# Early operands, value order, later value loads and wide weight decoding in an attention and FFN kernel

## The chip, the cores and the metric

The kernel runs on one core of one Trainium2 chip. The metric is the device time of one execution in microseconds. The engines have short names in the profile: PE is TensorE's matmul, PEld its weight load, DVE VectorE, ACT ScalarE, POOL GpSimd, SP the engine that issues DMAs.

## The reference: what is computed

Eight batches of eight heads, 576 tokens of 64 dimensions each, causal attention with a bias from a running sum; then a feed-forward network (FFN) with an ELU over all 4608 tokens (q comes scaled by 6.41 and k by 6.42):

```
scores = q @ k.T / sqrt(64)
cum    = cumsum(max(s, 0))                   # per batch and head
bias   = -(cum[:, None] - cum[None, :])
scores = where(causal, -1e9, scores + min(bias, 0))
p      = exp(scores - max(scores));  attn = p / (sum(p) + 1e-9)
x      = concat_heads(attn @ v)              # 4608 x 512
h      = x @ w_in                            # 512 x 2048
g      = where(h > 0, h, exp(min(h, 0)) - 1)
out    = g @ w_out                           # 2048 x 512
```

Two weight matrices reach the device as 64-bit numbers, and the kernel itself makes 32-bit numbers of them.

## The kernel before: how the work is tiled and ordered

**The plan.** All work is first recorded as operations (class Plan, L87). An operation has one or more ways (an engine and a cost in ns), what it reads and writes, and a priority. Plan.issue then puts them in order: the operation that can start first by the plan's costs, and among equals the one of lower priority number. It so fixes the order of every engine's instructions before the run, and each engine keeps it. Buffers of one tag are handed out in turn (N_ST = 2 buffers of tag st for keys of the early pairs, N_QS = 2 of tag qs for their queries); a load into a buffer waits until the work that used it before is done. In the first 60 us of the plan's time (FILL_T) transposes of the identity into a tile named scratch fill PE's gaps (L1569 to L1575): such a filler goes in when the next operation would start 350 ns later or more. They calculate nothing.

**The stages.** First decay_sums (L466) makes the running sums, in the tile aux, which is also written to aux_dram in DRAM. Then the early pairs (class Low): the first 320 tokens of batches 0 to 2, each batch as four pairs of heads, in native fp32. prepare_low (L824) loads keys (kl), queries (ql), and one row of decay into the keys' tile; scoring_low (L856) makes the scores (sc, L1101), masks them and takes the row's maximum on DVE (L1104), the exponential on ACT (L1109), the reciprocal of the sums (L1115) and the scaling by it (L1119 to L1124); weighing_low (L895) transposes the probabilities (trl, L904 and L925), copies them (tl) and multiplies by the values vs (avl). The result x_first is, for the first 256 tokens and a second chunk of 256, the operand of a native fp32 FFN (h at L1398, o at L1428).

After that come units: a pair of heads of a later batch with all 576 tokens, or the last 256 tokens of batches 0 to 2 (cut units); there are 20 full ones and 12 cut ones. Scores are again L1101. weighing (L1212) multiplies by the values, which are split in high and low 16-bit parts: heads (L1259) writes the products av (L1265), the two heads of the pair on the two 64-column halves of the array, three terms for each block of 128 keys, two for the last. In a full unit a block of keys meets 512, 448, 320, 192 and 64 columns of queries, in a cut one 256, 256, 256, 192 and 64. Meanwhile the FFN of the finished tokens runs in 16-bit parts (h at L1457, o at L1517), between the products of the units.

**Values.** group_values (L961) loads the values va of a full batch's pairs, four loads, each followed by its largest absolute value (peak, L595: DVE at L598, or ACT at L601 where a spare tile is at hand). Their priority is the unit's, less V_AHEAD.

**Weights.** Sixteen blocks of w_in and of w_out, 512 columns each. load_unit (L666) loads one (512 KB) into the ring w_raw of N_RAW = 4 places, ACT alters the high words (L684), DVE the low words (L687), DVE joins both to fp32 in wv (L690), and peak finds the largest; ACT's way uses the raw tile as its output. weight_scales makes a scale from four blocks' peaks, and split_unit (L699) splits wv in a scaled 16-bit high part (L414, L415) and a rest (DVE, L707).

The lines of load_unit that the change widens:

```
op(prio, [("ACT", act_s(512), lambda: act.activation(
    raw(1).bitcast(F32), raw(1).bitcast(F32), ...
op(prio, [("DVE-SB", 430.0, lambda: dve.tensor_scalar(
    raw(0), raw(0), 2.0**-29, 7.0, ALU.mult, ALU.min))],
```

Of the kernel before, what the change touches and what calls it, by code (L numbers as in the profile page):

```python
# [17 lines left out]
P = 128  # L18
# [17 lines left out]
V_AHEAD = 60  # L36
# [11 lines left out]
N_QS = 2  # L48
N_CUT, CUT = 3, 2
# [3 lines left out]
N_FREE = 0  # L53

# [288 lines left out]
def kernel(  # L343
# [114 lines left out]
    def low_keys(tag):  # L458

        k = plan.buf(sb, [P, 2, LOW], F32, f"kl_{tag}", tag="st", bufs=N_ST)  # L460
        return k, [("Pool-M", pool_1(2 * LOW), lambda: pool.memset(k.v[HB:], 0.0))]


    k_first, cleared = low_keys("first")

    def decay_sums():  # L466
# [25 lines left out]
        op(-10, [("DVE-SB", 2700.0, first)], [], [(aux, "row"), (k_first, "sums")])  # L492
# [70 lines left out]
    w_raw = plan.buf(sb, [P, N_RAW, 512, 2], U32, "w_raw", tag=f"wp_{NG - 1}")  # L563
# [11 lines left out]
    groups = [(b, False) for b in range(N_CUT, B)] + [(b, True) for b in range(N_CUT)]  # L575
    A_LOW, A_W = 0, N_CUT * (NP + 1)
# [3 lines left out]
    S_GROUP = S_LOW + 2 * N_CUT  # L580
# [85 lines left out]
    def load_unit(f, kind, src):  # L666

        prio = W_PRIO[f // W_GROUP] + f % W_GROUP
        a, n = src.shape[1], f"{'io'[kind]}{f}"
        place, value = weight(f, kind)  # L670
        at = A_W + f // W_GROUP * 2 * (W_GROUP + 1) + kind * (W_GROUP + 1) + f % W_GROUP
        r = (2 * f + kind) % N_RAW

        def raw(m):
            return w_raw.v[:, r, :, m]

        if wide:
            load(prio, lambda: w_raw.v[:, r].rearrange("p (a n) t -> p a (n t)", a=a),
                 lambda: src.bitcast(U32), [], [(w_raw, (r, 0)), (w_raw, (r, 1))], P * 4096,
                 urgent if f >= N_FREE else ())  # L680
# [3 lines left out]
            op(prio, [("ACT", act_s(512), lambda: act.activation(  # L684
                raw(1).bitcast(F32), raw(1).bitcast(F32),
                AF.Prelu, scale=2.0**-112, alpha=2.0**32))], [], [(w_raw, (r, 1))])
            op(prio, [("DVE-SB", 430.0, lambda: dve.tensor_scalar(  # L687
                raw(0), raw(0), 2.0**-29, 7.0, ALU.mult, ALU.min))],
               [], [(w_raw, (r, 0))])
# [966 lines left out]
```

## Time and profile before

| | us |
|---|---|
| runs | 1048.58, 1047.91, 1046.78 |
| median | 1047.91 |
| the profiled execution | 1049.47 |
| its span in the profile | 1047.7 |
| TensorE busy in the span | 1029.5 |
| VectorE busy in the span | 843.2 |

The granted clock of TensorE is 1.00 throughout. The span is the time from the first to the last instruction on the core; 1.77 us of the profiled execution lie around it. A row of the timeline gives the start, the length, engine, line, output and inputs, the count, and in brackets the wait before it; matmuls follow each other at less than the length shown, since they are pipelined and their ends are modelled. A row of groups gives the count, then busy time and mean length of one in ns, then idle time before them.

### The profile page before, as it was taken

Reading aid. Unit: us, or ns where it says so; the run is one execution under the profiler, and the core shown is the slowest. Engines: PE = TensorE matmul, PEld = TensorE weight load, DVE = VectorE, ACT = ScalarE, POOL = GpSimd, SP = SyncE. Lnnn points to the kernel's source line nnn. Section 1 sums busy time; section 2 is a strip of 40 time slices with the busy share of each in tenths; the row PEclk is TensorE's granted clock in tenths of the full one; section 3 lists DMA queues with packets and bytes.
Section 4 is the critical chain, followed back from the end, with each engine's and each line's share of the span. In section 5 each row is a group of like instructions: output and inputs, shape, how many; then the busy total and the mean of one; then the engine's idle time right before and its main releaser. Section 6 shows DMA issues by size and latency. Waiting matters only on the chain.

```text
span 1047.7 us, 21529 instructions
## 1 busy us (share of the span) xinstructions
PE 1029.5 (98%) x7161; PEld 710.2 (68%) x7161; DVE 843.2 (80%) x2142; ACT 619.8 (59%) x1475; POOL 428.7 (41%) x707
## 2 busy tenths in 40 slices
PE   9899999999999999999999999999999999999998
PEld 7556566667667676666676766666666676767665
DVE  7899958978898888789878998888888888885333
ACT  4788555655666666556676656656655566654232
POOL 4322415424545465446534555643433444441000
PEclk9999999999999999999999999999999999999999
DMA  7778025655666756658655855674666655663000
GB/s 235 247 227 240 26 74 142 131 148 115 139 129 147 171 122 129 134 122 174 128 132 119 186 129 124 137 175 94 147 131 155 131 130 123 142 108 73 1 21 21
DMA packets 277823, 137.76 MB, mean 131 GB/s; under 512 B 211768, under 2 KB 255056, under 8 KB 277712
## 3 DMA queue, kind: packets, MB, share of 16 engines
q1 hardware_dynamic: 277712, 136.39, 56.2%
q8 instruction: 57, 0.93, 0.4%
q14 instruction: 54, 0.44, 0.2%
HBM read 70.22 MB, written 9.88 MB: 76 GB/s over the span
## 4 chain that ended last, share of the span: by engine, by line
PE 83%; DVE 10%; DMA 3%; issue 2%; POOL 1%; ACT 1%; SPq 1%; POOLq 0%; DVEq 0%
PE h L1457 29%; PE o L1517 28%; PE sc L1101 9%; PE av L1265 5%; PE o L1428 4%; PE h L1398 4%; PE trl L925 1%; DVE p L1160 1%; PE scratch L1574 1%; PE avl L941 1%; DVE p L1104 1%; DMA vs<-in_vb_dram 1%; DVE peaks L598 1%; DVE wv L690 1%; DVE v L988 1%
## 5 line engine op out<-in xcount | busy, mean ns | idle before, releaser
L1457 PE MATMUL h<-x,wp 128*128 128x256 f16 x3072 | 380.6, 273 | 0.2 <-DVE x L1362 0.2
L1517 PE MATMUL o<-wp,gg 128*128 128x512 f16 x1536 | 362.1, 379 | 0.2 <-DVE gg L1496 0.2
L1457 PEld LDWEIGHTS <-wp 128*128 128x128 f16 x3072 | 286.6, 98 | 61.9 <-issue 7.5
L1517 PEld LDWEIGHTS <-gg 128*128 128x128 f16 x1536 | 144.9, 98 | 147.5 <-issue 2.8
L1109 ACT ACTIVATE p<-p,mn 128x192 f32<-128x192 f32 (+1 forms) x232 | 144.1, 621 | 73.0 <-DVE mn L1104 69.8
L1160 DVE SCALAR_TENSOR_TENSOR p<-p,sm,p 128x512 f16<-128x512 f32 (+3 forms) x221 | 159.8, 748 | 3.2 <-POOL p L1152 1.9
L1474 ACT ACTIVATE g<-h,cs 128x512 f32<-128x512 f32 x128 | 87.7, 685 | 109.1 <-PE h L1457 108.1
L1152 POOL TENSOR_SCALAR p<-p,sm 128x64 f16<-128x64 f32 (+3 forms) x125 | 81.1, 656 | 106.9 <-DVE sm L1115 70.0
L1104 DVE CUSTOM_DVE_ANT_0 p<-sc,maskw 128x192 f32<-128x192 f32 (+1 forms) x232 | 109.4, 481 | 18.2 <-PE sc L1101 15.9
L1491 ACT ACTIVATE gg<-h,wc 128x512 f16<-128x512 f32 x117 | 80.0, 684 | 68.0 <-DVE h L1487 67.2
L1101 PE MATMUL sc<-kh,qs 128*128 128x192 f32 (+2 forms) x272 | 112.3, 416 | 3.0 <-DVE mn L1104 3.0
L1496 DVE SCALAR_TENSOR_TENSOR gg<-h,wc,gg 128x512 f16<-128x512 f32 x128 | 95.5, 746 | 17.9 <-ACT gg L1491 17.4
L1487 DVE SCALAR_TENSOR_TENSOR h<-g,cs,h 128x512 f32<-128x512 f32 x128 | 96.2, 752 | 12.0 <-ACT g L1479 8.2
L1483 DVE TENSOR_SCALAR g<-g 128x512 f32<-128x512 f32 x77 | 36.2, 470 | 62.7 <-ACT g L1474 62.5
L1101 PE MATMUL sc<-k,q 128*128 128x192 f32 (+2 forms) x272 | 83.6, 310 | 0.6 <-DMA q<-qs 0.5
L1156 ACT ACTIVATE p<-p,sm 128x512 f16<-128x512 f32 (+3 forms) x104 | 59.0, 586 | 15.8 <-DVE sm L1115 14.9
L402 POOL TENSOR_SCALAR qs<-stq 128x512 fp32r<-128x512 f32 (+1 forms) x44 | 24.5, 558 | 100.9 <-PE sc L1101 66.2
L1101 PEld LDWEIGHTS sc<-kh,qs 128*128 128x128 f32 x272 | 51.6, 190 | 19.1 <-DVE mn L1104 4.7
L1398 PE MATMUL h<-x_first,wv 128*128 128x256 f32 x256 | 62.5, 382 | 0.6 <-ACT x_first L429 0.6
L1428 PE MATMUL o<-wv,gg 128*128 128x512 f32 x128 | 62.4, 595 | 0.0
L1265 PE MATMUL av<-T,v 128*64 128x256 f16 (+5 forms) x896 | 60.6, 286 | 0.2 <-DMA k<-aux_dram 0.2
L1265 PEld LDWEIGHTS <-v 128*64 128x64 f16 x896 | 44.9, 110 | 23.5 <-issue 8.6
(182 smaller groups left out, 1458.7 us busy)
## 6 DMA issues: line engine op xcount, KB each, us to landing
stk<-in_kT_dram SPq DMA_DIRECT2D x64, 288.0 KB
va<-in_vb_dram SPq DMA_DIRECT2D x32, 320.0 KB
stq<-in_qT_dram SPq DMA_DIRECT2D x40, 256.0 KB
w_raw<-in_w_in_dram SPq DMA_DIRECT2D x16, 512.0 KB
w_raw<-in_w_out_dram SPq DMA_DIRECT2D x16, 512.0 KB
out_dram<-ost SPq DMA_DIRECT2D x32, 256.0 KB
q<-qs SPq DMA_DIRECT2D x40, 128.0 KB
T<-p SPq DMA_TRANSPOSE x208
```

The source lines that it names most:

```text
L1101: pe_.matmul(view(sc.v[:, :cw]), l, r, start=n == 0, stop=n == len(pairs) - 1)
L1104: op(prio, [("DVE", 84 + dve_p(cw), lambda i=i, sc=sc: dve.tensor_tensor_reduce(pt.v[:, i * cw : (i + 1) * cw], sc.v[:, :cw], mv(i * cw, c ...
L1109: op(prio, [("ACT", 480 + w / 1.2, lambda: act.activation(pt.v[:, :w], pt.v[:, :w], AF.Exp, bias=mn.v[:, n - 1 : n], scale=-1.0, accum_out ...
L1160: ("DVE-SB", dve_2(n), lambda part=part: dve.scalar_tensor_tensor(part(t16, 1), own(part), sm.v[:, r], part(t16, 0), ALU.mult, ALU.subtract)),
L1265: pe_.matmul(av.v[w.h * HB : (w.h + 1) * HB, dst], w.values.v[:, w.h, kb, v], part(w, kb, m), start=kb == 0 and m == 0 and v == 0, stop=kb ...
L1398: op(main(ch), [("PE", pe4(TC), lambda m=m, c=c: pe_.matmul(hp.v[:, m], weight(2 * fp + m, 0)[1]()[:, c * P : (c + 1) * P], x_first.v[:, c ...
L1428: op(main(ch), [("PE", pe4(DM), lambda i=i, m=m: pe_.matmul(acc[i].v, gg.v[:, m, i * P : (i + 1) * P], weight(2 * fp + m, 1)[1](), start=f ...
L1457: pe_.matmul(hp.v[:, m], weight_part(f, 0, part)[1]()[:, c * P : (c + 1) * P], x.v[:, xx, c, o : o + TC], start=(c == 0 and i == 0), stop= ...
L1474: op(side, [("ACT", act_c(2 * TC) + 90, lambda: act.activation(gt.v, flat(hp.v), AF.Exp, scale=by(BACK)))], [hp, (cs[ch], g)], [gt])
L1487: op(side, [("DVE", dve_b(2 * TC), lambda: dve.scalar_tensor_tensor(flat(hp.v), gt.v, by(MINUS if sign[0] else FIRST), flat(hp.v), ALU.mul ...
L1496: op(side, [("DVE", dve_b(2 * TC), lambda: dve.scalar_tensor_tensor(flat(gg.v[:, 1]), flat(hp.v), down(), flat(gg.v[:, 0]), ALU.mult, ALU. ...
L1517: pe_.matmul(acc[i].v, gg.v[:, a, m, i * P : (i + 1) * P], weight_part(2 * fp + m, 1, part)[1](), start=(first and m == 0 and k == 0), sto ...
```

## The change

Six things are altered:

- Pairs 2 and 3 of batch 0 have their keys, queries and decay row in one tile of their own, early (of tag va), so that they are loaded at the start and wait for no buffer. Pairs 1 to 3 take the decay row from aux in SBUF; before, 2 and 3 took it from aux_dram.
- V_AHEAD is 30 in place of 60.
- A block of w_in and its block of w_out are decoded together, 1024 columns to an instruction, in a ring of two such blocks. The largest values come from one DVE reduction of both, or from two ACT instructions whose output goes to a tile w_abs, no longer to the raw tile.
- Blocks f and f + 1 of a kind are split together, 1024 columns to an instruction.
- The terms of av are written in alternating lengths, short then long, a long one last.
- N_WHOLE = N_CUT and N_URGENT = 1 name numbers that stood there already.

```diff
-V_AHEAD = 60
+V_AHEAD = 30
...
+N_EARLY, N_AUX, N_URGENT = 2, 4, 1
...
+    early = plan.buf(sb, [P, 2 * N_EARLY, 2 * LOW], F32, "early", tag="va", bufs=2)
+
+    def low_operands(n, tag, q_tag=True):
+        if 2 <= n < 2 + N_EARLY:
+            at = 2 * (n - 2)
+            return ((lambda part: (early, (n, part))), (lambda: early.v[:, at].rearrange("p (h t) -> p h t", h=2)),
+                    (lambda: early.v[:, at + 1]))
         k = plan.buf(sb, [P, 2, LOW], F32, f"kl_{tag}", tag="st", bufs=N_ST)
+        q = plan.buf(sb, [P, 2 * LOW], F32, f"ql_{tag}", tag="qs", bufs=N_QS)
...
-    w_raw = plan.buf(sb, [P, N_RAW, 512, 2], U32, "w_raw", tag=f"wp_{NG - 1}")
+    w_raw = plan.buf(sb, [P, N_RAW // 2, 2, 512, 2], U32, "w_raw", tag=f"wp_{NG - 1}")
+    w_abs = plan.buf(sb, [P, 512], F32, "w_abs")
...
+    def load_block(f, srcs):
...
-            op(prio, [("ACT", act_s(512), lambda: act.activation(
+            op(prio, [("ACT", act_s(1024), lambda: act.activation(
                 raw(1).bitcast(F32), raw(1).bitcast(F32),
-                AF.Prelu, scale=2.0**-112, alpha=2.0**32))], [], [(w_raw, (r, 1))])
-            op(prio, [("DVE-SB", 430.0, lambda: dve.tensor_scalar(
-                raw(0), raw(0), 2.0**-29, 7.0, ALU.mult, ALU.min))],
-               [], [(w_raw, (r, 0))])
-            op(prio, [("DVE-SB", 700.0, lambda: dve.scalar_tensor_tensor(
+                AF.Prelu, scale=2.0**-112, alpha=2.0**32))], [], highs)
+            op(prio, [("DVE-SB", 700.0, lambda: dve.tensor_scalar(
+                raw(0), raw(0), 2.0**-29, 7.0, ALU.mult, ALU.min))], [], lows)
+            op(prio, [("DVE-SB", 1240.0, lambda: dve.scalar_tensor_tensor(
                 value().bitcast(U32), raw(1), 3, raw(0),
...
+        ways = [("DVE", 140 + 1.04 * 1024, lambda: dve.tensor_reduce(
+            peaks.v[:, cols[0] : cols[1] + 1 : W_GROUP + 1], value(), mybir.AxisListType.X, ALU.max,
+            apply_absolute_value=True))]
+        def both():
+            for kind, col in enumerate(cols):
+                act.activation(w_abs.v, value()[:, kind], AF.Abs, accum_out=peaks.v[:, col : col + 1])
...
+    def split_units(f, kind):
...
+        scaled(prio, 1024, lambda: part(0), value, lambda: scales.v[:, col], [*places, (scales, at)], highs)
+        op(prio, [("DVE-SB", dve_2(1024), lambda: dve.scalar_tensor_tensor(
+            part(1), value(), scales.v[:, col], part(0), ALU.mult, ALU.subtract))],
+           [*places, (scales, at), *highs], lows)
...
-            src = aux if (b, j) == (0, 1) else aux_dram
+            src = aux if n < N_AUX else aux_dram
...
         def heads():
+            terms = [(kb, m, v) for kb in range(last + 1)
+                     for m, v in (((0, 0), (1, 0), (0, 1)) if kb < last else ((0, 0), (0, 1)))]
+            order, rest = terms[:1], sorted(terms[1:], key=lambda t: -columns(t[0]))
+            final = rest.pop(0)
+            while rest:
+                order.append(rest.pop())
+                if rest:
+                    order.append(rest.pop(0))
+            order.append(final)
...
-                for kb in range(last + 1):
+                for n, (kb, m, v) in enumerate(order):
                     dst = slice(wq - columns(kb), wq)
-                    for m, v in ((0, 0), (1, 0), (0, 1)) if kb < last else ((0, 0), (0, 1)):
-                        for w in pair:
```

The order of the engines' instructions changes with it. In a full unit the columns of the terms now run 512, 64, 512, 64, 448, 192, 448, 192, 448, 192, 320, 320, 320, 512. Fillers are 120 in number, 142 before. Three places, before and after.

SP, the loads behind the first pair's; va are full units' values, w_raw the weights, early the operands of pairs 2 and 3. Before:

```order
L390 DMA kl_1_131<-in_kT_dram 64x2x320
L390 DMA ql_1_139<-in_qT_dram 64x640
L390 DMA vs<-in_vb_dram 128x448
L390 DMA va_156<-in_vb_dram 128x640 x4
L390 DMA kl_1_131<-aux 1x2x320
L390 DMA aux_dram<-aux 64x576 x2
L390 DMA kl_2_232<-in_kT_dram 64x2x320
L390 DMA ql_2_239<-in_qT_dram 64x640
L390 DMA aux_dram<-aux 64x576
L390 DMA w_raw<-in_w_in_dram 128x4x256
```

The four va loads stand ahead of pair 2's operands (kl_2, ql_2). After, from the same place on SP:

```order
L391 DMA kl_1_131<-in_kT_dram 64x2x320
L391 DMA ql_1_139<-in_qT_dram 64x640
L391 DMA early<-in_kT_dram 64x2x320
L391 DMA early<-in_qT_dram 64x640
L391 DMA early<-in_kT_dram 64x2x320
L391 DMA early<-in_qT_dram 64x640
L391 DMA vs<-in_vb_dram 128x448
L391 DMA kl_1_131<-aux 1x2x320
L391 DMA aux_dram<-aux 64x576
L391 DMA early<-aux 1x2x320
```

The four operand loads of pairs 2 and 3 took the place of the four va loads, and the weights' loads moved down behind the rows of decay.

PE, from the last scores of pair 1 (sc_1_4) to the transposes of its probabilities (trl_1). Before:

```order
L1101 MATMUL sc_1_4_0_363<-kl_1_131,ql_1_139 128x320
L941 MATMUL avl_0_313<-tl_0_301,vs 64x64 x2
L1574 MATMUL scratch<-ident 128x128 x6
L1398 MATMUL h_0_391<-x_first,wv_366 128x256
L1574 MATMUL scratch<-ident 128x128 x21
L1101 MATMUL sc_2_0_0_431<-kl_2_232,ql_2_239 128x128
L904 MATMUL trl_1_434<-ident,pl_1_303 128x128
```

Pair 2's first scores stand behind 27 fillers and a product of the FFN. After, between the same two places on PE:

```order
L1141 MATMUL sc_1_4_0_345<-kl_1_131,ql_1_139 128x320
L981 MATMUL avl_0_298<-tl_0_288,vs 64x64 x2
L1141 MATMUL sc_2_0_0_355<-early 128x128
L1623 MATMUL scratch<-ident 128x128 x15
L944 MATMUL trl_1_394<-ident,pl_1_285 128x128
L1141 MATMUL sc_2_1_0_397<-early 128x192
L1623 MATMUL scratch<-ident 128x128 x2
```

The scores moved ahead of the fillers, of which 15 are left, and the FFN's first product comes later.

DVE, around the first reciprocal, of pair 0, up to pair 1's first mask (pl_1). Before:

```order
L598 TENSOR_REDUCE peaks<-vs 128x1
L598 TENSOR_REDUCE peaks<-va_156 128x1
L1115 RECIPROCAL sml_0_205<-sml_0_205 128x5
L1122 TENSOR_SCALAR pl_0_198<-pl_0_198,sml_0_205 128x128
L1122 TENSOR_SCALAR p_84<-p_84,sml_0_205 128x320
L598 TENSOR_REDUCE peaks<-va_156 128x1 x3
L1104 ISA pl_1_303,mn_1_0_304<-sc_1_0_0_294,masks 128x128
```

Four value peaks of full units stand there, three of them between the scaling and the mask. After, first the same place on DVE:

```order
L1155 RECIPROCAL sml_0_205<-sml_0_205 128x5
L1162 TENSOR_SCALAR pl_0_198<-pl_0_198,sml_0_205 128x128
L1162 TENSOR_SCALAR p_84<-p_84,sml_0_205 128x320
L613 TENSOR_REDUCE peaks<-vs 128x1
L1144 ISA pl_1_285,mn_1_0_286<-sc_1_0_0_278,masks 128x128
```

The peaks of va are gone from here; one of the early values vs stands in their place.

More of the change, by code (lines that the diff above doesn't have):

```diff
@@ L490, in lo @@
             return aux.v[:NB, 1]
-        op(-10, [("DVE-SB", 2700.0, first)], [], [(aux, "row"), (k_first, "sums")])
+        op(-10, [("DVE-SB", 2700.0, first)], [], [(aux, "row"), key("sums")])
         for cost, step in (
@@ L664, with value @@
     urgent = []
-    def load_unit(f, kind, src):
+    def load_block(f, srcs):
         prio = W_PRIO[f // W_GROUP] + f % W_GROUP
[L669 to L672, printed above, removed]
+        t, at = w_values[f // 2]
+        places = [weight(f, kind)[0] for kind in range(2)]
+        r = f % (N_RAW // 2)
+        cols = [A_W + f // W_GROUP * 2 * (W_GROUP + 1) + kind * (W_GROUP + 1) + f % W_GROUP for kind in range(2)]
+        def value():
+            return t.v[:, at + f % 2]
@@ L674, in raw, with word @@
         def raw(m):
[L675 removed]
+            return w_raw.v[:, r, :, :, m]
+        def word(m):
+            return w_raw, (r, m)
         if wide:
[L678 to L684, printed above, removed]
[L685 to L686 removed]
@@ L691, in load_unit @@
                 value().bitcast(U32), raw(1), 3, raw(0),
-                ALU.logical_shift_left, ALU.bitwise_or))], [(w_raw, (r, 0)), (w_raw, (r, 1))], [place])
+                ALU.logical_shift_left, ALU.bitwise_or))], lows + highs, places)
         else:
-            load(prio, lambda: value().rearrange("p (a n) -> p a n", a=a), lambda: src,
-                 [], [place], P * 2048, urgent)
-        peak(prio, 512, value, [place], at,
-             aside=(lambda: raw(0).bitcast(F32)) if wide else None, also=[(w_raw, (r, 0))] if wide else [])
@@ L701, in split_unit @@
+        if wide:
+            ways.append(("ACT", 2 * (480 + 512 / 1.2), both))
+        op(prio, ways, places, [(peaks, col) for col in cols] + [w_abs])
+    def split_units(f, kind):
         prio, at = SPLITS[f // W_GROUP] + 0.1 * (f % W_GROUP), 2 * (f // W_GROUP)
         col = slice(at + kind, at + kind + 1)
-        place, value = weight(f, kind)
-        (high, high_v), (low, low_v) = (weight_part(f, kind, m) for m in range(2))
-        scaled(prio, 512, high_v, value, lambda: scales.v[:, col], [place, (scales, at)], [high])
@@ L707, in split_unit, with value, part @@
-        op(prio, [("DVE-SB", dve_2(512), lambda: dve.scalar_tensor_tensor(
-            low_v(), value(), scales.v[:, col], high_v(), ALU.mult, ALU.subtract))],
-           [place, (scales, at), high], [low])
+        t, first = w_values[f // 2]
+        places = [weight(n, kind)[0] for n in (f, f + 1)]
+        highs, lows = ([weight_part(n, kind, m)[0] for n in (f, f + 1)] for m in range(2))
+        def value():
+            return t.v[:, first : first + 2, kind]
+        def part(m):
+            return w_parts[f // W_GROUP].v[:, f % W_GROUP : f % W_GROUP + 2, kind, m]
@@ L736 @@
         n = P * len(blocks) + HB * (not late)
-        low = not late and b < N_CUT
+        low = not late and b < N_WHOLE
         domain.append((at, at + n, S_LOW + 2 * b if low else S_GROUP + 2 * groups.index((b, late))))
```

80 lines of the change are left out of this document (45 added, 35 removed).

## The prediction

> **What bounds the kernel now.** I read the page first, then busy times by stretch, then PE's order of events in the first 60 us, and last the groups on DVE. The page:
>
> ```profile
> span 1047.7 us, 21529 instructions
> PE 1029.5 (98%) x7161; PEld 710.2 (68%) x7161; DVE 843.2 (80%) x2142; ACT 619.8 (59%) x1475; POOL 428.7 (41%) x707
> PE 83%; DVE 10%; DMA 3%; issue 2%; POOL 1%; ACT 1%; SPq 1%; POOLq 0%; DVEq 0%
> ```
>
> TensorE is busy 1029.5 of 1047.7 us; 18.2 us are idle. The change alters no product of scores, values or FFN. So it can gain in two ways only: by PE time that does no such work (idle, or filler transposes into "scratch"), or by making the same matmuls quicker. Where is the first kind? Busy time by stretch (length, then PE, PEld, DVE, ACT, POOL, the granted clock, DMA share, GB/s); the first six cuts are the starts of the reciprocals of successive early pairs:
>
> ```profile
> 14.18:25.81 11.63, 11.21 (x82) 8.07 (x80) 8.07 (x23) 7.38 (x22) 1.94 (x5) 1.00 0.83 266
> 25.81:38.12 12.31, 9.86 (x69) 6.91 (x67) 10.12 (x32) 8.55 (x27) 2.58 (x8) 1.00 0.78 242
> 38.12:47.93 9.81, 8.85 (x56) 5.80 (x55) 9.08 (x34) 7.86 (x23) 2.90 (x7) 1.00 0.85 265
> 47.93:58.47 10.54, 9.73 (x58) 6.24 (x57) 10.36 (x34) 9.12 (x26) 6.95 (x14) 1.00 0.66 191
> 58.47:71.27 12.80, 12.80 (x66) 8.03 (x66) 11.97 (x39) 11.16 (x32) 3.17 (x7) 1.00 0.79 239
> 71.27:112.10 40.83, 40.59 (x202) 25.78 (x202) 39.03 (x127) 33.38 (x92) 12.85 (x30) 1.00 0.70 201
> 112.10:150.00 37.90, 36.07 (x178) 21.29 (x176) 27.61 (x99) 21.21 (x60) 10.94 (x25) 1.00 0.08 20
> 150.00:950.00 800.00, 794.68 (x5731) 553.86 (x5731) 679.34 (x1683) 487.39 (x1141) 374.66 (x571) 1.00 0.62 137
> 950.00:1047.70 97.70, 93.53 (x656) 62.54 (x654) 37.04 (x62) 29.47 (x46) 2.23 (x4) 1.00 0.09 26
> ```
>
> From 150 to 950 us PE is full (794.68 of 800), so what other engines save there buys nothing. Idle lies in 14.18 to 58.47 (11.63−11.21, 12.31−9.86, 9.81−8.85, 10.54−9.73: together 4.64 us), in 112.10 to 150 (1.83) and at the tail (4.17). The early stretch is worse than its idle says, since part of its busy time is filler. PE's order there, and the fillers of 14.18 to 58.47 as one group:
>
> ```profile
> 11.52 4.75 PE L1574 MATMUL scratch<-ident 128*128 128x128 f32 x42
> 16.10 0.39 PE L1101 MATMUL sc<-kl,ql 128*128 128x128 f32 x2
> 24.39 2.46 PE L1574 MATMUL scratch<-ident 128*128 128x128 f32 x21
> 26.68 0.39 PE L1101 MATMUL sc<-kl,ql 128*128 128x128 f32 x2
> 26.90 0.27 PE L904 MATMUL trl<-ident,pl 128*128 128x128 f32 x1
> 37.14 1.47 PE L1574 MATMUL scratch<-ident 128*128 128x128 f32 x12
> 38.89 0.33 PE L904 MATMUL trl<-ident,pl 128*128 128x128 f32 x1 [0.28 <-POOL pl L1120]
> 48.89 0.30 PE L904 MATMUL trl<-ident,pl 128*128 128x128 f32 x1
> 59.82 0.27 PE L904 MATMUL trl<-ident,pl 128*128 128x128 f32 x1
> L1574 PE MATMUL scratch<-ident 128*128 128x128 f32 x77 | 10.4, 273 | 0.0
> ```
>
> The 273 ns of one is a modelled length that overlaps the next. From start to start it is (26.68−24.39)/21 = 0.109 us, so 77 fillers take 8.4 us. With the 4.64 idle, PE loses 13.0 of these 44.29 us. The pairs pass at the first transposes, 26.90, 38.89, 48.89 and 59.82, 10 to 12 us apart, while DVE is busy 10.12, 9.08 and 10.36 us of its 12.31, 9.81 and 10.54: DVE, 29.56 of 32.66, sets the pace, not PE. What takes DVE's time, and what else waits:
>
> ```profile
> 26.83 3.71 DMA vs<-in_vb_dram
> ```
> ```profile
> 15.07 2.25 DVE L598 TENSOR_REDUCE peaks<-va 128x1 f32<-128x640 f32 x3
> ```
> ```profile
> L598 DVE TENSOR_REDUCE peaks<-va 128x1 f32<-128x640 f32 x32 | 25.4, 810 | 0.7 <-DMA va<-in_vb_dram 0.7
> L707 DVE SCALAR_TENSOR_TENSOR wp<-wv,scales,wp 128x512 f16<-128x512 f32 x32 | 23.5, 763 | 0.0
> L690 DVE SCALAR_TENSOR_TENSOR wv<-w_raw 128x512 uint32<-128x512 uint32 x32 | 22.7, 712 | 1.0 <-ACT w_raw L684 0.8
> L687 DVE TENSOR_SCALAR w_raw<-w_raw 128x512 uint32<-128x512 uint32 x32 | 15.4, 495 | 0.0
> L598 DVE TENSOR_REDUCE peaks<-vs 128x1 f32<-128x448 f32 x8 | 4.9, 607 | 2.0 <-DMA vs<-in_vb_dram 1.9
> ```
>
> **The change part by part.** *Later values.* Three value peaks of full units stand on DVE at 15.07 us, 2.25 us in all, ahead of pair 1's first mask. With V_AHEAD at 30 the order puts the loads and these peaks behind the early pairs, so DVE loses 2.25 us where it sets the pace. They come back beside PE work that is full: nothing, with a bound of ±1 us for value loads that land later and for DMA ahead of them that lands sooner.
>
> *Wide weight instructions.* Two DVE instructions of 512 columns become one of 1024. The slope from the two value-peak rows is (810−607)/(640−448) = 1.06 ns a column, so 512 more columns cost 541 ns. The joined L690 saves 712−541 = 171 ns, the joined L707 763−541 = 222 ns. For L687 that slope is too steep (541 > 495), so the saving lies between 0 and 495; I take the share of L690, 24%, 120 ns. How many stand where, the windows of the three lines say (first L687 and L690 early, then L707 later):
>
> ```profile
> 14.18:58.47 44.29, 7.08 (x14) 1.00 0.78 241
> ```
> ```profile
> 14.18:58.47 44.29, 8.50 (x12) 1.00 0.78 241
> ```
> ```profile
> 112.10:150.00 37.90, 5.76 (x8) 1.00 0.08 20
> ```
>
> Early: 7 × 0.12 + 6 × 0.171 = 1.9 us. The eight splits between 112 and 150 us save 4 × 0.222 = 0.9 us where PE idles 1.83: I take 0.9, with bounds 0 and 1.8. From 58 to 112 us PE is as good as full, and the saving is free time of DVE. Weight peaks: either engine has cover, nothing.
>
> A wide instruction is also a longer obstacle. One of 1.25 us (712+541) stands where a mask or a reciprocal formerly waited for 0.71 at most, and it starts only when both loads of its block are there. Per pair that costs up to 0.54 us, over three pairs 1.6; I take a quarter, 0.4.
>
> *Operands at once.* Keys and queries of pairs 2 and 3 no longer wait for a buffer that the scores of pairs 0 and 1 free, and their decay row comes from SBUF rather than by a detour through DRAM. In PE's order the first scores of pair 2 move ahead of the 21 fillers. But the transposes that follow (26.90) wait for DVE's softmax of pair 1, so most of this is hidden behind DVE. On the chain also stands the load of a later pair's vs (3.71 us), for whose peak DVE waits (1.9 us over all eight); in both orders it follows operand loads that wait for a buffer, so I leave it. Between 0 and DVE's idle in the three periods (32.66−29.56 = 3.1 us) I take 0.3: DVE's work is what the period is nearest to. What is late next is DVE itself. Cover lost costs up to the same 0.3.
>
> Early sum: 2.25 + 1.9 − 0.4 + 0.3 = 4.0 us. Its lower bound is what the order itself lists: 142 fillers become 120, 22 × 0.109 = 2.4 us. Its upper one is all of DVE's saving and all its idle, 2.25 + 1.9 + 3.1 = 7.2. Since PE is full from 58 us on, what is won early stays won.
>
> *Alternating value products.* Both heads of a pair run side by side on two halves of the array. The rows: weight loads, one unit between runs of output products, unit lengths on the chain, and steady products:
>
> ```profile
> L1265 PEld LDWEIGHTS <-v 128*64 128x64 f16 x896 | 44.9, 110 | 23.5 <-issue 8.6
> ```
> ```profile
> 258.29 1.46 PE L1517 MATMUL o<-wp,gg 128*128 128x512 f16 x6
> 259.68 2.12 PE L1265 MATMUL av<-T,v 128*64 128x512 f16 x28
> ```
> ```profile
> 190.81 2.05 PE av L1265 x28
> 825.41 1.41 PE av L1265 x28
> 978.42 2.62 PE h L1457 x24
> 981.04 2.59 PE o L1517 x12
> ```
>
> 24 products of 256 columns in 2.62 us are 0.426 ns a column. The code gives a full unit 4544 columns per head, 1.94 us, against 2.05 measured: 0.11 over. A cut one has 3008, 1.28 against 1.41: 0.13 over. So the order of the terms can gain at most 20 × 0.11 + 12 × 0.13 = 3.8 us. I count none of it. Six output products take 6 × 2.59/12 = 1.30 us but hold PE from 258.29 to 259.68, 1.39, when values follow: the step into the narrow products costs 0.09 though a long matmul stands in front of it. That looks like the price of changing the array's width, once in, once out, and not of short matmuls in a row; alternation leaves both. The Trainium skill, "TensorEngine Tiling (Array Packing)", Key Properties, says that changing the tiling mode drains TensorE; by that the alternation gains nothing and the forecast stays, and the 0.09 us at a step in agrees.
>
> It may cost something: two 64-column products per unit, 64 × 0.426 = 27 ns each pair, now stand before long ones, and a weight load takes 110 ns. If the load is not hidden, 110−27 = 83 ns shows twice in each of 32 units: 5.3 us. The bounds are thus −3.8 and +5.3; I take 0, since the unit as it stands has steps of 27 ns, too, and is no more than 0.11 over. The same page, Restrictions, says that column tiling disables Fast Weight Load; if loads show behind short matmuls for that reason, the sum would be 1043.0 + 5.3 = 1048.3. No row here shows such a step alone.
>
> **Sum.** The profiled execution took 1049.47 us, 1.77 over its span and 1.56 over the median of 1047.91. 1049.47 − 4.0 − 0.9 = 1044.6, or 1043.0 at the median.
>
> **The rivals.**
> (a) *DVE and ACT give the head start back.* If every wide instruction delays the softmax beside it, the pairs lose 0.54 us on DVE and, taken alike, as much on ACT, four times: 4.3 of the 4.9 us, 1047.3. For it: ACT is busy 8.55 and 9.12 us of the periods, nearly as full as DVE, and the wide decode needs two loads. Against it: 2.25 us of value peaks leave whatever happens to the weights.
> (b) *Alternation pays.* If the 0.11 and 0.13 come from short matmuls in a row, 3.8 us more go: 1039.2. Against it stands the step in at 259.68.
> (c) *Weight loads show behind the 64-column products, slower.* Place: two steps in each of 32 units; price 5.3 us; with the early gain at its lower bound and nothing later 1047.91 − 2.4 + 5.3 = 1050.8. It decides if the early gain is under 3.2 us. For it: load 110 against 27 ns. Against it: loads of the other half can run meanwhile, and such steps stand in the unit already.
>
> **How the numbers follow.** Forecast 0.58, (a) 0.20, (b) 0.10, (c) 0.12. About 0.2%, 2.1 us, is what a measurement of this kernel can tell from no change. The forecast and (b) are faster by more: 0.68; (a), 0.6 us, within it: 0.20; (c) slower: 0.12. Low end: 1047.91 − 7.2 − 1.8 = 1038.9, and part of (b), 1038.0. High end: (c) reaches 1050.8; 1050.0 leaves most of it out.
>
> **What would show it.** In the profile after, the first transposes of pairs 1, 2, 3 and the next batch should come at about 23, 35, 44.5 and 56 us, the last 4 us before the 59.82 of now. The va peaks should be gone from before the first 60 us, wide L687's and L690's successors should take about 0.87 and 1.25 us, and from 150 us on PE should be as full. A value unit should take 2.05 and 1.41 us again. I am wrong if the transposes come at the old times (a), if units are 0.1 us shorter (b), or 0.17 longer (c), or if PE shows new idle after 150 us because values arrive late.

## The result and the profile after

The changed kernel takes 1056.75 us (median of 4 runs, 1054.67 to 1058.55) against 1048.24 for the one before beside it: ratio 1.0079, 95% interval 1.0064 to 1.0094. It is 8.5 us slower; 1043.0 was forecast. The profiled execution took 1054.67 us, 5.2 more than the 1049.47 of the profile before. The four runs took 1054.67, 1058.55, 1058.46 and 1055.04 us at a mean granted clock of 0.997, 0.992, 0.994 and 0.997: the profiled one is the first, so the clock that the second and third lost besides (0.003 to 0.005 of 1053 us, some 3 to 5 us) is not in its trace. The page after:

```profile
span 1052.9 us, 21378 instructions
PE 1031.1 (98%) x7139; PEld 703.1 (67%) x7139; DVE 831.8 (79%) x2095; ACT 623.3 (59%) x1465; POOL 426.4 (40%) x671
```

VectorE has 11.4 us less to do, as meant, and TensorE is busy for about as long. Busy time by stretch, cut as before up to 150 us (length, PE, PEld, DVE, ACT, POOL, granted clock, DMA share, GB/s):

```profile
14.18:25.81 11.63, 9.77 (x66) 6.60 (x66) 6.28 (x20) 6.34 (x20) 3.13 (x8) 1.00 0.74 241
25.81:38.12 12.31, 11.06 (x73) 7.30 (x72) 10.16 (x27) 8.72 (x25) 2.82 (x6) 1.00 0.75 237
38.12:47.93 9.81, 9.11 (x56) 5.82 (x55) 8.22 (x28) 8.94 (x24) 2.67 (x5) 1.00 0.68 238
...
112.10:150.00 37.90, 36.65 (x180) 21.98 (x179) 22.50 (x71) 21.48 (x60) 9.80 (x18) 1.00 0.12 36
150.00:250.00 100.00, 97.75 (x533) 65.56 (x532) 88.01 (x223) 55.09 (x133) 43.42 (x60) 1.00 0.60 145
250.00:300.00 50.00, 45.30 (x324) 31.50 (x323) 40.50 (x108) 28.35 (x68) 24.44 (x35) 0.93 0.57 119
```

The same two last stretches before:

```profile
150.00:250.00 100.00, 99.47 (x540) 69.71 (x540) 84.26 (x203) 58.62 (x145) 39.14 (x59) 1.00 0.59 142
250.00:300.00 50.00, 49.30 (x365) 33.85 (x363) 42.63 (x112) 30.35 (x72) 26.47 (x43) 1.00 0.61 137
```

Up to 150 us the kernel after is ahead (by the count of equal work below, 5.3 us at 153 us). From 150 to 250 PE idles 2.25 us in place of 0.53, and from 250 to 300 it idles 4.70 in place of 0.70, at a granted clock of 0.93. That is the place to look at. In PE's order after (start, length, line, out<-in, count, wait before it):

```profile
271.33 0.33 PE L1260 MATMUL av_None<-pc_None,vs_None 128*128 128x128 f32 x2
...
276.36 1.44 PE L1506 MATMUL h<-x,wp 128*128 128x256 f16 x6 [4.70 <-DVE x L1411]
```

The h at 276.36 is the 193rd in 16-bit parts: the first product of the third 16-bit chunk of tokens, "chunk 3" from here on. It needs x, which needs the last av_None, and that is issued only 5.0 us earlier. The same place before:

```profile
264.67 0.44 PE L1220 MATMUL av_None<-pc_None,vs_None 128*128 128x128 f32 x2 [0.16 <-DVE x L793]
...
267.34 1.46 PE L1517 MATMUL o<-wp,gg 128*128 128x512 f16 x6
...
268.81 1.47 PE L1517 MATMUL o<-wp,gg 128*128 128x512 f16 x6
270.47 2.78 PE L1457 MATMUL h<-x,wp 128*128 128x256 f16 x24 [0.18 <-DVE x L1362]
```

There 5.8 us passed between the two as well, but PE still had 12 h, 12 o and scores to fill them. After, no FFN product is left: all 192 h and 96 o of the chunks before have been issued. What DVE does in those 5 us:

```profile
271.70 0.48 DVE L431 COPY xs_None<-av_None 64x64 f32<-64x64 f32 x2 [0.18 <-PE av_None L1260]
...
272.94 0.22 DVE L1421 TENSOR_SCALAR cs<-scales,cs 128x4 f32<-128x4 f32 x1
273.20 0.64 DVE L1422 TENSOR_SCALAR cs<-cs 128x4 f32<-128x4 f32 x1
...
273.94 1.24 DVE L1424 TENSOR_TENSOR cs<-cs,wc 128x1 f32<-128x1 f32 x1
275.11 0.27 DVE L832 SCALAR_TENSOR_TENSOR x<-xs_None,scales,x 128x64 f16<-128x64 f32 x1
275.30 0.74 DVE L1200 SCALAR_TENSOR_TENSOR p<-p,sm,p 128x512 f16<-128x512 f32 x1
275.97 0.34 DVE L1411 TENSOR_SCALAR x<-x,cs 128x512 f16<-128x512 f16 x1
```

It is busy 5.00 of the 5.40 us from 271.00 to 276.40; the chain from av_None to x is DVE's. And the loss doesn't end with the wait (stretches after; the clock is the third number from the end):

```profile
271.00:276.40 5.40, 0.70 (x7) 0.61 (x6) 5.00 (x15) 1.01 (x3) 3.25 (x5) 0.89 0.94 184
276.40:281.00 4.60, 4.60 (x23) 3.47 (x22) 2.13 (x8) 1.63 (x4) 0.00 (x0) 0.50 0.49 33
281.00:287.00 6.00, 6.00 (x52) 5.18 (x52) 5.11 (x11) 4.23 (x11) 3.45 (x4) 0.91 0.65 161
```

For 4.60 us the granted clock is 0.50, then 0.91 over 6.00: 4.60 × 0.50 + 6.00 × 0.09 = 2.8 us of full-speed work. "TensorE: Matmul & The Clock Gate" in the Trainium skill, Part 1 "Seeing it yourself", shows the clock being halved 5.2 us after a last matmul. Here it took less: the last av_None ends at 271.7, and the clock reads 0.50 from 275.2 us on, 3.5 us later, with PE still empty, up to 282.0.

A count over the whole trace comes near the sum. Give each PE instruction other than fillers the tenth percentile of the start-to-start steps of its kind in the profile before, add these up as "work", and compare when equal work is done: after is 5.3 us ahead at 100 us of work, 2.7 ahead at 200, and 6.3 behind at 210, which is chunk 3; at the end it is 5.2 behind. So −2.7 + (4.70 − 0.18) + 2.8 = +4.6, of 5.2. It doesn't close: the step at chunk 3 is 9.0 us, 1.7 more than the wait and the clock, and 1.1 of it comes back later.

### The profile page after: what moved, and what is told of

Same layout as the page of the kernel before. It is cut to its first block, busy times and chain, and to the rows that moved or that the text cites. A ratio compares the mean times of both kernels' runs of the same rounds, so it can differ in the third digit from the quotient of the medians.

```text
span 1052.9 us, 21378 instructions
## 1 busy us (share of the span) xinstructions
PE 1031.1 (98%) x7139; PEld 703.1 (67%) x7139; DVE 831.8 (79%) x2095; ACT 623.3 (59%) x1465; POOL 426.4 (40%) x671
## 5 line engine op out<-in xcount | busy, mean ns | idle before, releaser
L1200 DVE SCALAR_TENSOR_TENSOR p<-p,sm,p 128x512 f16<-128x512 f32 (+3 forms) x231 | 164.2, 731 | 3.2 <-POOL p L1192 2.1
L1192 POOL TENSOR_SCALAR p<-p,sm 128x512 f16<-128x512 f32 (+3 forms) x116 | 72.8, 634 | 109.0 <-DVE sm L1155 73.5
L424 POOL TENSOR_TENSOR qs<-stq,qs 64x512 fp32r<-64x512 f32 (+1 forms) x46 | 51.5, 1120 | 33.2 <-ACT qs L405 21.2
L1141 PEld LDWEIGHTS sc<-k,q 128*128 128x128 f32 x272 | 51.9, 191 | 4.8 <-issue 1.0
```

The lines of the kernel that those rows point to most:

```text
L1141: pe_.matmul(view(sc.v[:, :cw]), l, r, start=n == 0, stop=n == len(pairs) - 1)
L1192: ("Pool", 160 + 1.04 * n, lambda part=part: pool.tensor_scalar(part(t16, 0), own(part), sm.v[:, r], 1.0, ALU.mult, ALU.mult)),
L1200: ("DVE-SB", dve_2(n), lambda part=part: dve.scalar_tensor_tensor(part(t16, 1), own(part), sm.v[:, r], part(t16, 0), ALU.mult, ALU.subtract)),
```

## Experiments

In the expectations, theory A puts the loss on the wait at chunk 3, brought about by values that come late through a shared buffer; B puts it on the wide weight instructions; B1 and B2 put it on one half of those. Each kernel was timed in five rounds; a ratio is to runs of the kernel before on the same chip, and costs are counted by it (0.001 is 1.05 us). "Chunk 3" is the start of its first product in the profiled execution, with PE's wait there. That one execution need not be like the median one: early_alone's took 1056.74 us and act_wide's 1051.76, 3.7 and 4.2 more than their medians, both with a halved clock long before chunk 3.

| kernel | us | ratio to before (95%) | chunk 3 | wait |
|---|---|---|---|---|
| before | 1048.24 | | 270.5 | 0.18 |
| after | 1056.75 | 1.0079 (1.0064–1.0094) | 276.4 | 4.70 |
| v_ahead_alone | 1048.83 | 0.9996 (0.9985–1.0007) | 269.5 | 0 |
| plain_order | 1055.87 | 1.0075 (1.0063–1.0087) | 278.6 | 4.70 |
| early_alone | 1053.02 | 1.0053 (1.0034–1.0072) | 276.4 | 2.99 |
| wide_alone | 1055.39 | 1.0058 (1.0043–1.0073) | 277.4 | 0 |
| own_buffer | 1053.46 | 1.0053 (1.0039–1.0068) | 272.3 | 0 |
| narrow_weights | 1050.02 | 1.0017 (1.0005–1.0030) | 271.5 | 0.22 |
| narrow_decode | 1052.57 | 1.0034 (1.0017–1.0050) | 269.7 | 0 |
| act_wide | 1047.56 | 0.9992 (0.9979–1.0005) | 276.3 | 0 |
| dve_wide | 1046.98 | 0.9984 (0.9971–0.9996) | 270.9 | 0 |
| narrow_own | 1049.70 | 1.0012 (1.0001–1.0023) | 271.7 | 0 |
| one_pair_early | 1054.68 | 1.0051 (1.0034–1.0068) | 271.1 | 0 |
| pe_kept_busy | 1055.35 | 1.0066 (1.0047–1.0085) | 280.5 | 3.15 |
| clock_kept | 1051.24 | 1.0028 (1.0015–1.0041) | 277.5 | 0.36 |
| constants_held | 1114.47 | 1.0630 (1.0602–1.0659) | 276.8 | 4.01, ahead of scores |

**One part undone or alone.** The old order of the terms in the kernel after:

```diff
-                order.append(rest.pop())
...
+                for kb in range(last + 1):
+                    for m, v in ((0, 0), (1, 0), (0, 1)) if kb < last else ((0, 0), (0, 1)):
```

> The changed kernel with the terms of the value products in their former order; every engine's order is else the same. Theory A and B: the same time as the changed kernel, 1053 to 1059 us, units of 2.05 and 1.42 us. If the alternating lengths cost time (weight loads seen behind the 64-column products), up to 5 us less.

Measured 1.0075 against 1.0079: the alternation does nothing. The unit's row after says so too:

```profile
606.75 2.05 PE av L1314 x28
```

V_AHEAD alone, in the kernel before:

```diff
-V_AHEAD = 60
+V_AHEAD = 30
```

> The kernel before with V_AHEAD 30 alone. The first values still load at the start, as their buffer is free there; the order leaves 4.7 us of FFN work ahead of chunk 3. Theory A: no difference, 1047 to 1050 us. Rival (V_AHEAD is what makes the values late): 1052 us or more.

0.9996: nothing. It doesn't move the first values either. What does is the tile early. It is of tag va, which has two buffers; vs, the values of the early pairs, holds one of them to the end of those pairs, and early takes the other. The next values go into the place of vs, so their loads wait for the last early pair (SP's queue after; before, the first four were issued at 7.52):

```profile
160.47 2.02 SPq L391 DMA_DIRECT2D va<-in_vb_dram  x4
163.07 2.33 SPq L391 DMA_DIRECT2D va<-in_vb_dram  x4
```

Eight reductions then stand on DVE where pairs and FFN want it, the first and the last of them:

```profile
164.76 0.80 DVE L613 TENSOR_REDUCE peaks<-va 128x1 f32<-128x640 f32 x1
176.77 0.82 DVE L613 TENSOR_REDUCE peaks<-va 128x1 f32<-128x640 f32 x1
```

The first value unit starts at 201.1 us (before: 190.7). Two kernels take this apart: early with a buffer of its own, and the early operands alone in the kernel before.

```diff
-    early = plan.buf(sb, [P, 2 * N_EARLY, 2 * LOW], F32, "early", tag="va", bufs=2)
+    early = plan.buf(sb, [P, 2 * N_EARLY, 2 * LOW], F32, "early")
```

> The changed kernel, with the tile early in a buffer of its own and no longer in the two that vs and the full units' values va rotate in; so the first four va are loaded and reduced at the start again. Theory A (the first value group came only when vs's buffer was free, at 160 us, so that eight value reductions and four splits fell into DVE's full stretch after 160 us, the units came 7 to 10 us late, and the FFN ran out of work before its chunk 3 at 271 us): the 4.7 us wait of h on x and the stretch of halved clock behind it are gone, some 2 us of the early gain are given back to the four reductions, 1044 to 1049 us. Theory B (the 1024-column weight instructions are the obstacle): nothing changes, 1053 to 1059 us.

```diff
+    early = plan.buf(sb, [P, 2 * N_EARLY, 2 * LOW], F32, "early", tag="va", bufs=2)
+    def low_operands(n, tag, q_tag=True):
...
-            src = aux if (b, j) == (0, 1) else aux_dram
+            src = aux if n < N_AUX else aux_dram
```

> The kernel before with the early operands alone (own tile in the values' buffers, decay rows from SBUF); V_AHEAD 60, weights by 512, old order of the value terms. Its order of TensorE leaves 1.7 us of FFN work ahead of chunk 3. Theory A: a wait of about 3 us there and some halved clock behind it, against 2 to 3 us won early: 1048 to 1053 us. Theory B: faster than before by the early gain, 1044 to 1046 us.

With a buffer of its own the wait at chunk 3 is gone, as A says, but the time is 1053.46, not A's. The four va loads are back at the start (10.62 us), and early's decay rows now follow them on SP's queue, at 15.32 and 19.58 in place of 11.89 and 14.80; at 10 us of PE work this kernel is 4.4 us behind before. Its last early reciprocal comes at 158.2. The early operands alone cost 0.53%, 5.6 us; they have the wait, shorter, and with it a lower clock:

```profile
276.35 1.44 PE L1471 MATMUL h<-x,wp 128*128 128x256 f16 x6 [2.99 <-DVE x L1376]
```
```profile
276.40:281.00 4.60, 4.60 (x30) 3.73 (x30) 2.72 (x11) 2.17 (x6) 0.00 (x0) 0.69 0.92 195
```

In the second row the clock is 0.50 up to 279.2 us and 1.00 from there. The pairs are not late here: the last early reciprocal comes at 141.0 us, 6.4 sooner than before, and yet chunk 3 begins 5.9 us later. And the clock reads 0.50 once more, from 16.4 to 26.7 us. PE waits there for the decay row of pair 1, 1.78 us; in after it waits too, in before it doesn't:

```profile
14.27 0.46 PE L1141 MATMUL sc<-kl,ql 128*128 128x128 f32 x2 [0.92 <-DMA kl<-aux]
```

Ahead of this product stand 24 fillers, where 42 stood before. In five of the thirteen profiles with early operands (early_alone, plain_order, narrow_decode, dve_wide, clock_kept) the clock is 0.50 behind this wait, for 3.4 us in the other four; in after's it stays at 1.00. So the early operands put the clock at risk in a second place, which no theory here counted; what that costs in the mean isn't shown.

So A is a part of it and not all. The wide weights by themselves, in the kernel before:

```diff
-            op(prio, [("ACT", act_s(512), lambda: act.activation(
+            op(prio, [("ACT", act_s(1024), lambda: act.activation(
...
-            op(prio, [("DVE-SB", 700.0, lambda: dve.scalar_tensor_tensor(
+            op(prio, [("DVE-SB", 1240.0, lambda: dve.scalar_tensor_tensor(
```

> The kernel before with the 1024-column decode and split alone; the values load at the start, V_AHEAD 60, no early tile. Its order leaves 4.7 us of FFN work ahead of chunk 3. Theory B (wide weight instructions delay the early pairs behind other work, so the attention path ends later): the last early pair ends 5 us or more later than before and the time is 1050 to 1054 us. Rival (all the loss comes from the late values): 1045 to 1048 us, faster by what VectorE saves.

They cost 0.58%, 6.1 us, with no wait at chunk 3. By equal work this kernel is 2.0 us behind at 80, 6.3 at 120 (185 us of its time) and 7.7 at 160: the loss is made beside the early pairs and just behind them. Its last early reciprocal comes at 157.2 us, 9.7 later than before, as B has it (5 us or more); the time is over B's 1054. The trace of after has the same wide instructions in another order, and shows what they can do there. The reciprocals of two successive pairs after, and what stands just ahead of the second:

```profile
57.30 0.18 DVE L1155 RECIPROCAL sml<-sml 128x5 f32<-128x5 f32 x1
57.42 1.22 DVE L712 SCALAR_TENSOR_TENSOR wv<-w_raw 128x1024 uint32<-128x1024 uint32 x1
72.77 1.22 DVE L712 SCALAR_TENSOR_TENSOR wv<-w_raw 128x1024 uint32<-128x1024 uint32 x1
74.44 0.18 DVE L1155 RECIPROCAL sml<-sml 128x5 f32<-128x5 f32 x1
```

17.1 us from one to the next, where it was 12.8 before (58.47 to 71.27). The two L712 shown are the first and the last of four in this period: 4096 columns joined, where five L690 joined 2560 before. Each instruction is cheaper by the column, but the order puts more of them ahead of a pair. In wide_alone it is less of the same: 15.4 us from 62.76 to 78.14, with three wide joins, 3072 columns. In after DVE so serves the weights, PE gets FFN products early, and the pairs fall behind. One group up to 152 us, before and then after:

```profile
L1398 PE MATMUL h<-x_first,wv 128*128 128x256 f32 x128 | 32.4, 384 | 0.6 <-ACT x_first L429 0.6
```
```profile
L1447 PE MATMUL h<-x_first,wv 128*128 128x256 f32 x154 | 39.1, 384 | 0.4 <-DVE x_first L431 0.4
```

26 native FFN products are done earlier, about 6 us (ten of them take 2.43), while the last early reciprocal comes at 151.9 in place of 147.4. PE's lead of 5 us is FFN work taken from the store that fills the gap ahead of chunk 3. That is after's case: in wide_alone 132 of these products are done by 152 us, 4 more than before.

**Which half of the wide work.** In the kernel after, 512 columns again for decode, bounds and splits (narrow_weights); for decode and bounds alone (narrow_decode); for DVE's decode alone (act_wide); for ACT's decode alone (dve_wide). The last two:

```diff
-            op(prio, [("DVE-SB", 700.0, lambda: dve.tensor_scalar(
+            for kind in range(2):
+                op(prio, [("DVE-SB", 430.0, lambda kind=kind: dve.tensor_scalar(
```
```diff
-            op(prio, [("ACT", act_s(1024), lambda: act.activation(
+            for kind in range(2):
+                op(prio, [("ACT", act_s(512), lambda kind=kind: act.activation(
```

and of the first two, narrow_decode only the second line pair, narrow_weights both:

```diff
-    def split_units(f, kind):
+    def split_unit(f, kind):
...
-    def load_block(f, srcs):
+    def load_unit(f, kind, src):
```

> The changed kernel with the weights decoded, reduced and split by 512 columns as before; early still shares the values' buffers, so the first two value groups are still loaded together after the early pairs. Its order of TensorE leaves 5.1 us of FFN work between the last product that chunk 3 needs and chunk 3, where the changed kernel's leaves none. Theory A in its form that the empty stretch ahead of chunk 3 is what costs: no such wait, 1043 to 1047 us. Theory A in the form that late values cost DVE time whatever the order: 1050 us or more. Theory B (wide weight instructions): 1043 to 1047 us.

> The changed kernel with the weights decoded and reduced by 512 columns as before; split by 1024, early operands, V_AHEAD 30 and late values stay. Its order leaves 5.5 us of FFN work ahead of chunk 3. Theory A: no wait there, early gain in part kept, 1046 to 1050 us. Rival (late values cost in any order): 1052 us or more.

> The changed kernel with the two decoding steps of VectorE by 512 columns again; ScalarE's decode, the reductions and the split stay at 1024, all else as changed. Theory B1 (VectorE's long instructions stand in the pairs' way): the last reciprocal of the early pairs comes at 139 to 144 us in place of 151.9, and the time is 1048 to 1052 us. Rival B2 (ScalarE's long instruction does it): it stays at 150 to 155 us and 1054 to 1058 us.

> The changed kernel with ScalarE's decode by 512 columns again; VectorE's two decoding steps, the reductions and the split stay at 1024. Theory B1: the last reciprocal of the early pairs stays at 150 to 155 us, 1054 to 1058 us. Rival B2: it comes at 139 to 144 us, 1048 to 1052 us.

Narrow weights leave 1.8 us of the loss: 1050.02 is above the 1047 of A and B, and at the edge of A's second form, by which late values cost in any order. narrow_decode misses A's range and, at 1052.57, lies in that of its rival, again that late values cost in any order. Against this stand the next two kernels, whose values come late as well (from 156 and 151 us) and which lose nothing. Either half made narrow by itself takes all of the loss away: B1 and B2 both fall, since neither long instruction does harm alone. The last early reciprocals, 149.4 in act_wide and 145.3 in dve_wide, lie between what B1 and B2 expected. Yet with both halves narrow (narrow_decode) 3.6 us are lost, so the length of these instructions doesn't decide; that the order made with them does is likely, and not shown. dve_wide is the one kernel that beats before, by 0.16% (0.04 to 0.29%), which as the best of fourteen may be luck. Its chunk 3 has FFN products to wait with:

```profile
267.90 1.46 PE L1567 MATMUL o<-wp,gg 128*128 128x512 f16 x6
269.46 1.47 PE L1567 MATMUL o<-wp,gg 128*128 128x512 f16 x6
270.95 3.13 PE L1507 MATMUL h<-x,wp 128*128 128x256 f16 x27
```

In act_wide's profile chunk 3 begins at 276.3, as late as in after, but with 4.7 us of FFN products and scores ahead of it, and without a wait. That a late chunk 3 costs nothing by itself doesn't follow, since the clock of this execution was 0.50 from 34.0 to 40.8 and from 197.8 to 201.2 us; where chunk 3 begins in a median run of act_wide isn't known. Counted in this way from PE's order, the work (FFN products and scores) between the last av_None and chunk 3 is 0.0 us in after and plain_order, 1.7 in early_alone and 4.7 or more in the ten kernels of this list that wait 0.22 us or less: the waits of 4.70, 4.70 and 2.99 are what the cover leaves of some 4.7 us.

Two more tries at a better kernel: narrow weights with a buffer for early, and narrow weights with the old terms and one early pair in place of two.

```diff
-    early = plan.buf(sb, [P, 2 * N_EARLY, 2 * LOW], F32, "early", tag="va", bufs=2)
+    early = plan.buf(sb, [P, 2 * N_EARLY, 2 * LOW], F32, "early")
...
-    def load_block(f, srcs):
+    def load_unit(f, kind, src):
```

> The changed kernel with weights by 512 and early in a buffer of its own, so that the first values load at the start. Theory A: from the last reciprocal of the early pairs to chunk 3 it takes 120 to 125 us (133 with late values), and the time is 1044 to 1049 us, below that of narrow_weights (1050.0); part of what the late values cost is given back at the start, where four reductions and 1.3 MB of loads come back. Rival (late values cost nothing once the weights are narrow): 1049 to 1052 us.

```diff
-N_EARLY, N_AUX, N_URGENT = 2, 4, 1
+N_EARLY, N_AUX, N_URGENT = 1, 2, 1
...
-    def load_block(f, srcs):
+    def load_unit(f, kind, src):
```

> Weights by 512, old order of the value terms, V_AHEAD 30, and only pair 2 of batch 0 in early, decay rows of pairs 2 and 3 from DRAM; a try at a version that beats both. Its order leaves 7.6 us of FFN work ahead of chunk 3. Theory A: values are late here too, so 1047 to 1051 us. If the pair stage alone decides: 1043 to 1046 us.

The first is no better than narrow_weights by more than the intervals tell, and its 1049.70 fits the rival, that late values cost nothing once the weights are narrow. The second is a miss: it has no wait at chunk 3, and by equal work it falls from 2.0 to 5.9 us behind between 250 and 350, with waits of PE for DVE that no theory here foresaw.

**The wait and the clock.** Transposes of the identity that nothing reads, put on PE into the empty stretch of the kernel after; they calculate nothing. First 40, which write the bank of av_None:

```diff
+                if (u.b, u.j) == (3, 3):
+                    def keep_busy():
+                        for _ in range(40):
+                            pe_.transpose(av.v[:, P : 2 * P], ident, ident)
+
+                    op(-2000, [("PE", 1.0, keep_busy)], [av], [])
```

> The changed kernel, every engine's order as it is, with 40 more transposes of the identity on TensorE (into unread columns of a bank) right behind the last product that chunk 3 waits for, where TensorE was empty for 4.7 us. Theory A (a date set by the attention path, plus a halved clock after the empty stretch): chunk 3 still starts at about 276 us, but the clock stays at 1.00 behind it, and 2.5 to 3 us go: 1052.5 to 1054.5 us. Rival (the low clock has nothing to do with the empty stretch): 1055 to 1058 us.

The clock stayed at 1.00 behind it, but DVE's copies of av_None waited for the transposes, so chunk 3 came 4.1 us later and the gain was eaten: 1055.35 is a time of the rival's, but the clock speaks against the rival. So 28 were put behind those copies:

```diff
+                        for _ in range(28):
+                            pe_.transpose(av.v[:, P : 2 * P], ident, ident)
+
+                    op(-2000, [("PE", 1.0, keep_busy)], [av, (x, 0), (x, 1)], [])
```

> The kernel after, with 28 transposes of the identity, whose result nothing reads, put on PE into the empty stretch ahead of chunk 3; every engine's other instructions stand in the order of after, and DVE waits for none of the transposes. Chunk 3's first product still comes at about 276 us, since what it waits for is on DVE. If the halved clock behind the empty stretch costs what the windows show (4.60 us at 0.50 and 6.00 us at 0.91): the clock reads 1.00 there and the time falls by 2 to 3 us, to 1053 to 1055. If the clock is made good behind it in any case, because DVE sets the pace there too: 1055.5 to 1058.

PE's order, and the clock by stretch, at the same place:

```profile
272.41 0.33 PE L1260 MATMUL av_None<-pc_None,vs_None 128*128 128x128 f32 x2
273.82 3.28 PE L1280 MATMUL av_None<-ident 128*128 128x128 f32 x28 [1.07 <-DVE xs_None L1339]
277.46 0.82 PE L1512 MATMUL h<-x,wp 128*128 128x256 f16 x6 [0.36 <-DVE x L1417]
```
```profile
276.40:281.00 4.60, 4.24 (x39) 3.58 (x38) 3.97 (x15) 1.76 (x5) 0.00 (x0) 1.00 0.36 88
281.00:287.00 6.00, 6.00 (x54) 5.03 (x52) 5.84 (x13) 3.98 (x11) 4.50 (x5) 1.00 0.68 162
```

The six h take 0.82 us in place of 1.44. Chunk 3 is no earlier, and the kernel takes 1051.24: from 1.0079 to 1.0028 of before, 5.3 us of the 8.5. The mechanism is as expected and its size is larger, 5.3 in place of 2 to 3. By equal work in the profiles this kernel is 1.1 us behind after at 200 us and 1.5 ahead at 210, so 2.6 us are won just behind chunk 3, as the clock's 2.8; some 3 more come between 350 and 600, where after has waits of under 1 us that this kernel has not or has shorter. Whether these follow from the slow clock isn't settled; pe_kept_busy wins 2.6 us over the same stretch, though its chunk 3 is later than after's. Over all runs the median of the mean clock is 0.9955 in after and 0.9995 in clock_kept, which is some 4 us of 1053: by that most of the 5.3 us is clock, and not all of it behind chunk 3, where the profile shows 2.8. The last kernel held back the preparation of a later chunk's constants (L1421 to L1424, in the list of DVE's rows above):

```diff
-                    rank = (start + GAP if o.filler else start, o.prio)
+                    rank = (start + (GAP if o.filler else o.hold), o.prio)
...
+        if ch == 6:
+            o.hold = HELD
```

> The kernel after, with the four DVE instructions that prepare chunk 6's constants held back in the order, so that they no longer stand between chunk 3's last inputs and its scaling; up to chunk 3 the order is that of after. If the loss is the wait at chunk 3 and the halved clock behind it: those four instructions take 2.4 us there, so the wait falls from 4.70 us to 2 to 3 us, chunk 3 begins at about 274 us, the clock behind it is low for less time or not at all, and the time is 1052 to 1054.5. If the loss lies elsewhere (small waits before 250 us, or the order behind chunk 3): 1055.5 to 1058, whatever the wait there does.

It fails twice. Chunk 3 begins at 276.75, no earlier, and PE's wait is 4.01 for a mask ahead of it. A mask now stands in the chain, and an instruction that took 0.25 us in after takes longer:

```profile
273.21 1.31 DVE L417 TENSOR_SCALAR x<-xs_None,scales 128x64 f16<-128x64 f32 x1
275.41 0.62 DVE L1144 CUSTOM_DVE_ANT_0 p<-sc,maskw 128x448 f32<-128x448 f32 x1
```

And the order behind chunk 3, which the hold changed as well, loses 60 us between 440 and 520, with the clock at 0.50 for much of it. Of the share of the wait it tells nothing.

## Why the prediction was wrong, point by point

- *Early sum, 4.0 us: right in place, and right in size only for PE's work.* First transposes of pairs 1, 2, 3 and the next batch, after:

```profile
24.21 0.33 PE L944 MATMUL trl<-ident,pl 128*128 128x128 f32 x1
35.41 0.33 PE L944 MATMUL trl<-ident,pl 128*128 128x128 f32 x1
45.94 0.30 PE L944 MATMUL trl<-ident,pl 128*128 128x128 f32 x1
58.62 0.27 PE L944 MATMUL trl<-ident,pl 128*128 128x128 f32 x1
```

  They are 2.7, 3.5, 2.9 and 1.2 us earlier (forecast: 4 at the last, where it failed; that they hardly move there is what rival (a) named). By equal PE work after is 5.2 us ahead at 40. The difference between the two measures is the first sign of what went wrong: the lead was FFN work, less and less the pairs.
- *Later values, 2.25 us early and "nothing" later: failed twice.* V_AHEAD moves nothing; the shared buffer does, so the 2.25 us belong to the tile early, which alone cost 5.6 us where 2.25 and 0.3 of gain were counted. And the reductions did not come back beside work that hides them: they stand on DVE where it is full, and the first value unit comes 10 us later.
- *Wide weight instructions, 1.9 + 0.9: failed.* The lengths were forecast well:

```profile
L747 DVE SCALAR_TENSOR_TENSOR wp<-wv,scales,wp 128x1024 f16<-128x1024 f32 x16 | 20.6, 1287 | 0.0
L712 DVE SCALAR_TENSOR_TENSOR wv<-w_raw 128x1024 uint32<-128x1024 uint32 x16 | 19.9, 1245 | 0.5
L710 DVE TENSOR_SCALAR w_raw<-w_raw 128x1024 uint32<-128x1024 uint32 x16 | 11.5, 716 | 0.4 <-DMA w_raw<-in_w_out_dram 0.4
```

  1.25 us for L712 as worked out, 0.72 for L710 (0.87), and still the change alone costs 6.1 us. The price was put on instructions; their place in the order was left out, and the last early pair moved by 9.7 us with it. Rival (a) saw the direction, that they would delay the softmax, and stopped at 58 us and at 4.3 us.
- *"Since PE is full from 58 us on, what is won early stays won": the step that failed.* PE is full, but of two kinds of work. The attention chain, set by DVE, dates chunk 3; FFN products are the store that covers for it. After did more of the store early and the chain later, the store ran out at 271 us, and an empty stretch of 4.70 us and the halved clock behind it, 2.8 us, took the lead and more. The sum had no term for the clock; transposes that keep it up in that stretch brought back 5.3 of the 8.5 us (clock_kept). The sentence on what would prove it wrong, new idle of PE after 150 us, came true.
- *Alternation, 0, with units of 2.05 and 1.41 again: right.* Units take 2.05 to 2.06 and 1.41 to 1.42. Rivals (b) and (c) fall. The Trainium skill, "TensorEngine Tiling (Array Packing)", Key Properties, says that a change of the tiling mode drains TensorE, and no run here speaks against it.
- *The chances.* The only way to slower, 0.12, was (c). That an edit changes the whole order, so that its parts don't add, had no chance at all; measured alone the parts come to 0, +5.6 and +6.1 us, and together to 8.3.

What stays open: why wide_alone, own_buffer and one_pair_early lose 5 us or more without the wait at chunk 3, by many small waits; why either half of the wide decode is harmless, while both wide lose 8.3 us and both narrow 3.6; and the later 3 us of clock_kept.

## What to carry to other kernels

A full engine doesn't mean that a head start is kept: ask which of its work is a store that covers for a chain on another engine, and whether the change spends the store early. Where a planner makes the order, price an edit by the dates that it gives to the chain, not by the length of its instructions, and try its parts alone. A tile put into a shared ring delays whatever comes next in that ring, so look for who holds the other place, and for how long.

## What the hardware showed

A stretch of 4.70 us without a matmul was followed by a granted clock of 0.50 from 275.2 to 282.0 us in after, and for 3.4 us in plain_order; one of 2.99 us (early_alone) by 0.50 for 3.4 us; one of 3.15 us (pe_kept_busy) by none, 1.00 throughout. In act_wide's profile waits of 2.22 us up to 34.7 and of 1.89 us up to 197.4 went with 0.50, too, for 6.8 us from 34.0 and 3.4 us from 197.8. So the length of a wait alone doesn't tell whether the clock falls, and a wait can cost half as much again as it lasts, or more. Transposes that calculate nothing kept the clock at 1.00 as real work does, and they were worth 5.3 us here where the wait itself could not be shortened.
